# One step of the first chunk's normalisation at each turn of the attention loop, in place of each third

## The chip, the core and the metric

The kernel runs on one core of a Trainium2 chip, in one launch. The metric is device microseconds (us) of that core, from one execution of the whole program; every time below is of that kind. The engines are called by the names of the profile: PE multiplies matrices, DVE is the vector engine, ACT the scalar engine, POOL is GpSimd, and SP issues transfers. Each engine runs its own list of instructions strictly in order, and waits on semaphores for the others.

## What is computed

Three parts follow each other. The first is causal attention with a decay, for 4 batches and 8 heads of 576 positions and 64 channels; its output is 4 x 576 rows of 512 channels. The second takes the real part of a two-dimensional Fourier transform, normalises each row, and runs a feed-forward layer. The third mixes tokens and channels. In short:

```python
scores = scale * q @ k.T + decay          # causal, 32 heads of 576 x 576
x = softmax(scores) @ v                   # -> (4, 576, 512)
u = x + real(fft(fft(x, axis=1), axis=2))
un = (u - mean(u)) / sqrt(var(u) + 1e-6)
x = u + relu(un @ w_ch1) @ w_ch2
theta = x @ w_theta
y = w_tok_r @ (x * cos(theta)) + w_tok_i @ (x * sin(theta))
out = (x + y) + relu((x + y) @ w_ch)
```

## The kernel before, in words

The sum `u` is kept whole in fast memory, with the 512 channels on 4 x 128 partitions and the 2304 rows along the free axis. The feed-forward part cuts these rows into 6 chunks of 384 (`CH`), numbered 0 to 5.

**The attention loop** (`phase1`) walks over the heads n = -1 to 33. In each round it keeps three heads in flight: the scores of head n+1 (`score_units`, matrix products at lines 215 and 216; on DVE the row minimum at 220 and 223; the exponential on ACT at 228; a scaling on DVE and POOL at 240), the transposes of head n-1 (`turn_units`, PE line 258, copies at 262 and 264), and the product with the values of head n-2 (`av_units`, PE line 276). When a pair of heads is complete, ACT copies it out (`evac_pair`, lines 291 to 307, with a small transfer and the two vector instructions 305 and 307). When a batch is complete, its Fourier sums are computed by `fft_units`: the products at lines 360 and 371 from the tiles `eh`, `el`, `oh`, `ol` (made at 333 to 342), then those at 388, and the result goes to `u`.

A round of the loop has 6 turns, and each turn calls `pull()`, which advances three generators by one step where it may: the rows of `evac_pair`, the normalisation `norm`, and the Fourier sums `fft`. Chunk 0 lies in batch 0 and is complete long before; its normalisation generator is made in the round n = 29, after the third batch's Fourier sums have been drained. Rounds 29 to 33 have 30 turns.

**The normalisation** of one chunk (`norm_units`, then `norm_end`) has 20 steps: three sums on POOL (lines 637 to 639); the mean by PE (643) and the differences on DVE (645); squares on ACT (648) and their sums on POOL (649, 651), twice; a wait of eight empty steps; the variance by PE (656) and the root on ACT (663); two empty steps; the reciprocal on DVE (666) and its spread over the partitions by PE (668); and then four steps, each with a product on DVE (675), a copy on ACT (676) and a remainder on DVE (677). The last two make the tile `un`. What is left of the generator when the loop ends is drained in one piece (`for _ in norm`).

**The weights** of the feed-forward part come as 64-bit numbers, and `decode` makes two float32r parts of each (`wf`): on DVE lines 519, 523, 527, 531, 534 and, for most, 535; on ACT 520, 522, 532; on POOL 536 and 538. `load(k)` queues the two halves of the weights of unit k. From round 31 on, `fill(2)` advances this queue by two steps in each turn.

**The feed-forward part** (`phase2`) first drains the last batch's Fourier sums and then runs its units: `ffn1` (PE line 688, 12 products, from `un` and `wf`; the two parts of `h` at 693 on ACT and 694 on DVE) and `ffn2` (PE line 702, the sum into `u` at 710 on DVE). The first two `ffn1` need `un` of chunk 0 and the weights of units 0 and 1.

What order the instructions have on each engine is not only that of the code: a scheduler orders them by the code's order, its own costs and `high_priority` marks, so a moved step shifts its neighbours on every engine too.

Of the kernel before, what the change touches and what calls it, by code (L numbers as in the profile page):

```python
# [31 lines left out]
C1 = 6.28125  # L32
C2 = 2.0 * math.pi - 6.28125
MAGIC = 12582912.0
# 64-bit weights, read by their high words as float32 patterns: the least normal float32 (squared)
# and the largest that 12 bits hold.
LEAST2 = (1.125 * 2.0**-15) ** 2
MOST = 122876.0
G = 4
# [2 lines left out]
def f(ap):  # L42
    return ap.bitcast(F32)


class Net:
# [31 lines left out]
    def bank_t(self):  # L78
        return self.pst.tile([128, 1024], F32, tag="t", name="pt")

# [1 line left out]
    def p1_open(self):  # L82
        nc, tc = self.nc, self.tc
        self.p1f, self.p1a, self.p1b, self.pu0 = (ExitStack() for _ in range(4))
# [330 lines left out]
    def phase1(self):  # L415
        pair, heads = self.p1_open()
        NH = B * H
        pairs, heads, raws = {0: pair}, dict(enumerate(heads)), {}
        T, EO, fft = None, None, None
        self.tick = 0  # L420
        rows, norm = iter(()), iter(())

        def pull():
            nonlocal fft
            next(rows, 0)
            self.tick += 1
            if self.tick % 3 == 0:
                next(norm, 0)
            if (self.tick % 5 or n > 24) and fft is not None and next(fft, 0) == 0:
                fft = None  # L430

        for n in range(-1, NH + 2):
            a = self.score_units(heads[n + 1], (n + 1) % 2) if n + 1 < NH else iter(())
            prep = iter(())
            if n + 2 < NH:
                p, g = divmod(n + 2, 2)
                if n >= 0:
                    heads[n + 2] = dict(pair=pairs[p], g=n + 2)
                    prep = self.prep_units(n + 2, pairs[p], raws.pop(n + 2), heads[n + 2])
                if g == 1 and p + 1 < B * NP:  # L440
                    pairs[p + 1] = self.load_pair(p + 1)
            if n + 3 < NH:
                raws[n + 3] = self.load_head(n + 3)
            c = iter(())
            m = n - 2
            if m >= 0:
                pm, gm = divmod(m, 2)
                hm = pm % NP
                if gm == 0:
                    T = self.bank_t()  # L450
                    if hm == 0:
                        E = self.c1.tile([128, 2, S], F32, tag="E", name="E", bufs=2)
                        O = self.c1.tile([128, 2, S], F32, tag="O", name="O", bufs=2)
                        EO = (E, O)
                c = self.av_units(heads[m], gm, T)
            t = self.turn_units(heads[n - 1]) if 1 <= n <= NH else iter(())
            if n == NH - 1:
                self.p1a.close()
                self.p2_open()
                self.load(0)  # L460
                self.load(1)
            k = n - 2
            if 0 <= k < 4:
                for j in range(2):
                    self.load_dft(2 * k + j, f(heads[n]["hi"][0:1, 0, 0:2]))
            if n == NH - 3:
                while fft is not None:
                    pull()
                t1 = self.c1.tile([128, 2, CH], F32, tag="E", name="uc1", bufs=2)
                t2 = self.c1.tile([128, 2, CH], F32, tag="O", name="uc2", bufs=2)  # L470
                t3 = self.c1.tile([128, 2, CH], F32, tag="yh", name="s12", bufs=1)
                t4 = self.c1.tile([128, 2, CH], F32, tag="yl", name="sq", bufs=1)
                t5 = self.c1.tile([128, 4], F32, tag="zh", name="rs", bufs=1)
                norm = self.norm_units(0, ((t1, t2), t3[:, 0], t3[:, 1], t4, t5))
            live = True
            while live:
                live = False
                for g_ in [(a, c, t)[i] for i in [2, 1, 0]]:
                    if next(g_, 0) is None:
                        live = True  # L480
                next(prep, 0)
                pull()
                if n >= NH - 1:
                    self.fill(2)
            for _ in prep:
                pass
            if m >= 0 and gm == 1:
                for _ in rows:
                    pass
                rows = self.evac_pair(EO[0], EO[1], hm, T)  # L490
                next(rows)
                if hm == NP - 1:
                    fft = self.fft_units(pm // NP, *EO)
        for _ in norm:
            pass
        self.p1b.close()
        for _ in rows:
            pass
        self.pt.close()
        self.pso = self.ctx.enter_context(self.tc.tile_pool(name="pso", bufs=2, space=PSUM))  # L500
        return fft

# [1 line left out]
    def decode(self, place, src, n):  # L504
        nc, w = self.nc, self.x1
        raw = w.tile([128, 512, 2], I32, tag="raw", name="raw", bufs=2)
        nc.sync.dma_start(
            raw[:, 0:n], src.bitcast(I32).rearrange("p (n t) -> p n t", t=2)
        )
        self.nraw += 1  # L510
        me = self.nd
        self.nd += 1
        low, high = raw[:, 0:n, 0], raw[:, 0:n, 1]
        yield
        dst = place()
        a = w.tile([128, 512], F32, tag="sq", name="a", bufs=3)[:, 0:n]
        t = w.tile([128, 512], I32, tag="t", name="t", bufs=3)[:, 0:n]
        square, tail = f(dst[:, 0]), f(dst[:, 1])
        nc.vector.tensor_scalar(a, f(high), MOST, -MOST, ALU.min, ALU.max)  # L519
        nc.scalar.activation(dst[:, 1], low.bitcast(U32), AF.Copy, scale=2.0**-52)  # L520
        self.nraw -= 1
        nc.scalar.activation(dst[:, 0], a, AF.Square)
        nc.vector.tensor_scalar(
            t, a.bitcast(I32), 3, 0x3FFFFFF8, ALU.logical_shift_left, ALU.bitwise_and
        )
        yield
        nc.vector.scalar_tensor_tensor(
            t, a.bitcast(I32), -0x40000000, t, ALU.bitwise_and, ALU.bitwise_or
        )
        yield  # L530
        nc.vector.scalar_tensor_tensor(a, square, LEAST2, f(t), ALU.is_ge, ALU.mult)  # L531
        nc.scalar.copy(dst[:, 0], a)
        yield
        nc.vector.tensor_scalar(t, a.bitcast(I32), -0x00800000, None, ALU.bitwise_and)  # L534
        (nc.gpsimd if me in [4, 6] else nc.vector).tensor_tensor(dst[:, 1], tail, f(t), ALU.mult)  # L535
        nc.gpsimd.tensor_tensor(a, a, f(dst[:, 0]), ALU.subtract)  # L536
        yield
        nc.gpsimd.tensor_tensor(dst[:, 1], a, tail, ALU.add)
        yield
# [45 lines left out]
        while self.step(g) is None:  # L585
            pass

# [1 line left out]
    def p2_open(self):  # L589
        nc, tc = self.nc, self.tc  # L590
        self.pw, self.px2 = ExitStack(), ExitStack()
        self.x1 = self.pw.enter_context(tc.tile_pool(name="x1", bufs=1, side="right"))
        self.wf = {}
        self.queue, self.raws, self.loads = deque(), deque(), {}
        self.nraw = self.nd = 0
        self.active = 3
# [188 lines left out]
        while self.queue:  # L785
            self.fill(1)

# [1 line left out]
    def load_big(self, into, name, k):  # L789
        def place():  # L790
            into.append(self.wtile("x" if name == "wth" else "w"))
            return into[-1]

        self.later(self.decode(place, self.i[name][k], 512))
# [326 lines left out]
```

## Time and profile before

| what | value |
|---|---|
| time, median of 3 runs (lowest to highest) | 1077.78 us (1076.75 to 1079.5) |
| span of the profiled execution, from the first to the last instruction | 1078.3 us |
| PE busy, matrix products | 1007.1 us (93%) |
| DVE busy | 770.6 us (71%) |
| POOL busy | 515.0 us (48%) |
| ACT busy | 480.9 us (45%) |
| chain that ended last | PE 65%, DVE 24%, issue 6%, ACT 3%, POOL 2% |

The profile gives the span of one profiled execution and no other time for it; it lies 0.5 us above the median of the runs. Busy time is what an engine spends inside instructions, and matrix products overlap, so a busy PE need not be at its peak. The chain that ended last is followed back from the last instruction, at each step to what released it. A share over the whole span mixes stages with different limits; the stage around the change is read apart, in the rows below.

### The profile page before, as it was taken

The page shows a single profiled execution, that of the slowest core. Times are in us where ns is not written, and L with a number is a line of the kernel's source. Part 1 is how long each engine was busy: PE and PEld are TensorE (multiplying, and loading weights), DVE is VectorE, ACT ScalarE, POOL GpSimd, SP SyncE. Part 2 cuts the span into 40 slices and gives each one's busy share as a digit, 9 for nine tenths or more (in the row PEclk, how much of TensorE's full clock was granted, in tenths as well). Part 3 has the DMA queues.
Part 4 walks back from the last instruction along what each step waited for, and adds up shares of the span by engine and source line. Part 5 has one row for each costly group of instructions (what it writes and reads, how often), then busy time and mean ns, then how long its engine had stood idle before and what let it go on. Part 6 is the DMA issues. An engine that isn't in the chain of part 4 may idle for free.

```text
span 1078.3 us, 16568 instructions
## 1 busy us (share of the span) xinstructions
PE 1007.1 (93%) x5880; PEld 896.2 (83%) x5880; DVE 770.6 (71%) x1767; ACT 480.9 (45%) x1151; POOL 515.0 (48%) x560
## 2 busy tenths in 40 slices
PE   3999999999997898999999999999789999999998
PEld 1676777766765687899999999989688999999998
DVE  7678988877778878766454555589989675666654
ACT  5677866755646443242222222234334453434331
POOL 5666757646566447443222222236637463635321
PEclk9989999998899889799999999999989999999999
DMA  4453223322204111011111111113221000000001
GB/s 157 136 167 116 95 89 101 101 75 71 93 25 137 40 59 40 1 40 40 40 40 40 40 40 40 40 64 103 67 64 59 1 1 34 12 23 23 12 35 44
DMA packets 21910, 64.78 MB, mean 60 GB/s; under 512 B 3286, under 2 KB 6614, under 8 KB 21828
## 3 DMA queue, kind: packets, MB, share of 16 engines
q1 hardware_dynamic: 18100, 59.36, 16.7%
q0 software_dynamic: 3008, 3.20, 1.2%
q10 hardware_dynamic: 720, 1.18, 0.3%
q8 instruction: 46, 0.75, 0.3%
q14 instruction: 36, 0.29, 0.1%
HBM read 58.83 MB, written 4.87 MB: 59 GB/s over the span
## 4 chain that ended last, share of the span: by engine, by line
PE 65%; DVE 24%; issue 6%; ACT 3%; POOL 2%; ACTq 0%; DVEq 0%; POOLq 0%
PE pa L688 11%; PE pt L276 9%; PE pb L258 7%; PE pb L702 6%; PE po L702 5%; PE pb L901 4%; PE pa L912 4%; PE pa L865 3%; PE pa L215 3%; PE pa L216 3%; PE pb L388 3%; PE po L901 3%; DVE wf L535 2%; DVE a L519 2%; DVE a L531 2%
## 5 line engine op out<-in xcount | busy, mean ns | idle before, releaser
L688 PE MATMUL pa<-un,wf 128*128 128x384 f32 x1152 | 228.4, 348 | 6.6 <-ACT un L676 5.6
L688 PEld LDWEIGHTS pa<-un,wf 128*128 128x128 f32 x1152 | 210.7, 197 | 10.0 <-ACT un L676 6.3
L536 POOL TENSOR_TENSOR a<-a,wf 128x512 f32<-128x512 f32 x40 | 67.6, 1691 | 192.9 <-DVE t L534 174.7
L702 PE MATMUL pb<-h,wf 128*128 128x384 f32 x660 | 138.6, 342 | 11.3 <-DVE u L710 9.7
L694 DVE SCALAR_TENSOR_TENSOR h<-pa,h 128x384 fp32r<-128x384 f32 x96 | 53.0, 552 | 122.6 <-ACT h L693 122.5
L276 PE MATMUL pt<-PT,v 128*128 128x320 f32 (+4 forms) x448 | 132.2, 402 | 0.5 <-ACT O L292 0.5
L702 PEld LDWEIGHTS pb<-h,wf 128*128 128x128 f32 x660 | 117.6, 190 | 14.4 <-DVE u L710 12.1
L228 ACT ACTIVATE P<-pa,mn 64x512 f32<-64x512 f32 (+4 forms) x192 | 97.6, 513 | 62.3 <-DVE mn L223 56.0
L693 ACT ACTIVATE h<-pa 128x384 fp32r<-128x384 f32 x96 | 46.7, 488 | 174.8 <-PE pa L688 174.7
L702 PE MATMUL po<-h,wf 128*128 128x384 f32 x492 | 107.2, 347 | 15.3 <-DVE u L710 11.3
L702 PEld LDWEIGHTS po<-h,wf 128*128 128x128 f32 x492 | 89.5, 194 | 17.5 <-DVE u L710 12.6
L240 POOL TENSOR_SCALAR P<-P,rz 128x128 f32<-128x128 f32 (+3 forms) x128 | 83.0, 664 | 43.7 <-DVE rz L237 30.3
L258 PE MATMUL pb<-ident,P 128*128 128x128 f32 (+2 forms) x480 | 101.7, 292 | 1.5 <-POOL P L240 1.2
L215 PE MATMUL pa<-hi 128*64 128x512 f32 (+2 forms) x192 | 79.6, 421 | 20.7 <-ACT P L228 10.9
L901 PE MATMUL pb<-wtk,z 128*128 128x288 f32 x513 | 97.0, 294 | 0.0
L258 PEld LDWEIGHTS pb<-ident,P 128*128 128x128 f32 (+2 forms) x480 | 60.0, 141 | 42.6 <-issue 19.2
L891 POOL TENSOR_TENSOR z<-kra,z 128x256 fp32r<-128x256 f32 x72 | 53.8, 767 | 86.8 <-ACT z L890 86.8
L276 PEld LDWEIGHTS pt<-PT,v 128*128 128x128 f32 (+1 forms) x448 | 75.3, 197 | 23.5 <-issue 8.0
L220 DVE TENSOR_REDUCE mn<-pa 64x1 f32<-64x512 f32 (+3 forms) x128 | 59.8, 479 | 37.9 <-PE pa L216 36.9
L901 PEld LDWEIGHTS pb<-wtk,z 128*128 128x128 f32 x513 | 79.2, 188 | 0.0
L901 PE MATMUL po<-wtk,z 128*128 128x288 f32 x351 | 75.1, 295 | 1.0 <-POOL z L891 1.0
L215 PEld LDWEIGHTS pa<-hi 128*128 128x128 f32 (+1 forms) x192 | 36.2, 189 | 35.1 <-ACT P L228 14.5
(197 smaller groups left out, 2063.8 us busy)
## 6 DMA issues: line engine op xcount, KB each, us to landing
raw<-in_qk SPq DMA_DIRECT2D x31, 576.0 KB, 3.7
raw<-in_wf SPq DMA_DIRECT2D x32, 512.0 KB, 3.6
v<-in_vp SPq DMA_DIRECT2D x16, 640.0 KB, 4.4
raw<-in_wtk SPq DMA_DIRECT2D x18, 288.0 KB, 2.9
out<-ob SPq DMA_DIRECT2D x12, 288.0 KB, 2.1
dft<-in_dft POOLq DMA_DIRECT2D x8, 346.0 KB, 3.7
raw<-in_wth SPq DMA_DIRECT2D x4, 512.0 KB, 3.7
raw<-in_wch SPq DMA_DIRECT2D x4, 512.0 KB, 3.5
```

The costliest lines, as they stand in the source:

```text
L215: nc.tensor.matmul(t[:m, 0 : b - a], hi[:, 1, n0 : n0 + m], hi[:, 0, a:b], start=True, stop=False)
L220: nc.vector.tensor_reduce(mn[:m, i : i + 1], ps[:m, 0:n0], mybir.AxisListType.X, ALU.min)
L228: nc.scalar.activation(P[:m, POFF[i] + a : POFF[i] + b], t[:m, 0 : b - a], AF.Exp, bias=lowest, scale=-1.0, accum_out=zs[:m, i + k : i + k ...
L240: (nc.vector if k in [3] else nc.gpsimd).tensor_scalar(P[:m, o : o + w], P[:m, o : o + w], rz[:m, k : k + 1], 1.0, ALU.mult, ALU.mult)
L258: nc.tensor.transpose(ps[:kw, off % 512 : off % 512 + qw], src, self.ident[:qw, :qw])
L276: nc.tensor.matmul(T[:, 256 + a : 256 + hi_q], v[:kw, j, g, :], PT[:kw, PTOFF[j] + a - 128 * j : PTOFF[j] + hi_q - 128 * j], start=(g == 0 ...
L536: nc.gpsimd.tensor_tensor(a, a, f(dst[:, 0]), ALU.subtract)
L688: nc.tensor.matmul(ps[:, 0:CH], t[:, l, 128 * d : 128 * d + 128], un[r][:, d], start=n == 0, stop=n == 11)
L694: nc.vector.scalar_tensor_tensor(h[:, 1], ps[:, 0:CH], 0.0, f(h[:, 0]), ALU.max, ALU.subtract)
L702: nc.tensor.matmul(outs[d], t[:, l, 128 * d : 128 * d + 128], h[:, r], start=k % G == 0 and n == 0, stop=k % G == G - 1 and n == 2,)
L891: nc.gpsimd.tensor_tensor(z[:, 1], t, f(z[:, 0]), ALU.subtract)
L901: nc.tensor.matmul(acc[k][th], z[:, l, 128 * k : 128 * k + 128], self.wtk[kt][:, r, 288 * th : 288 * th + 288], start=first and i == 0 and ...
```

## The change

`pull()` now advances the normalisation of chunk 0 at each turn and no longer at each third. Only chunk 0 has its normalisation there; those of the chunks 1 to 5 are advanced by the queue of `phase2`. In 30 turns the generator made 10 of its steps before, and the rest was drained behind the loop. Now all 20 are made by the turn 20 of 30, so nothing is left to drain. The rest of the diff takes out comments. One line less in `pull()` moves every line behind it up by one: what is line 688 in the profile of before is 687 in the changed kernel.

```diff
         def pull():
             nonlocal fft
             next(rows, 0)
             self.tick += 1
-            if self.tick % 3 == 0:
-                next(norm, 0)
+            next(norm, 0)
             if (self.tick % 5 or n > 24) and fft is not None and next(fft, 0) == 0:
                 fft = None
```

The scheduler makes of this another order on every engine, from the scores of head 30 to the second chunk of the feed-forward part; behind that the orders are equal again. Three places of it follow. A name `pt` is the sum of a pair of heads, `pa` and `pb` are other banks, `po` an output bank of `ffn2`.

On PE, the mean of chunk 0 in the kernel before stands behind the first scores of head 31 (`q_97`):

```order
L215 MATMUL pa<-hi 64x64
L216 MATMUL pa<-kl,q_97 64x64
L643 MATMUL pb<-s_3187,mean 128x384
L215 MATMUL pa<-hi 128x512
L216 MATMUL pa<-kl,q_97 128x512
```

and now, within the scores of head 30 (`q_96`):

```order
L215 MATMUL pa<-hi 128x256
L216 MATMUL pa<-kl,q_96 128x256
L642 MATMUL pb<-s_3187,mean 128x384
L215 MATMUL pa<-hi 128x128
L216 MATMUL pa<-kl,q_96 128x128
```

The mean moved one head forward, ahead of the last score product of head 30.

On PE at the end of the attention, before (the last L276 belong to head 31):

```order
L656 MATMUL pb<-mean,s_3187 128x1 x3
L276 MATMUL pt<-PT,v 128x256
L276 MATMUL pt<-PT,v 128x320
L276 MATMUL pt<-PT,v 128x128
L276 MATMUL pt<-PT,v 128x320 x2
L276 MATMUL pt<-PT,v 128x192
L276 MATMUL pt<-PT,v 128x64
L668 MATMUL pb<-ident,rs 128x128 x3
L688 MATMUL pa<-un,wf 128x384 x24
L702 MATMUL po<-h,wf 128x384 x7
L360 MATMUL pb<-dft,eh 128x258 x2
```

and now:

```order
L687 MATMUL pa<-un,wf 128x384 x8
L276 MATMUL pt<-PT,v 128x256
L276 MATMUL pt<-PT,v 128x320
L276 MATMUL pt<-PT,v 128x128
L276 MATMUL pt<-PT,v 128x320 x2
L276 MATMUL pt<-PT,v 128x192
L276 MATMUL pt<-PT,v 128x64
L687 MATMUL pa<-un,wf 128x384 x14
L701 MATMUL po<-h,wf 128x384 x4
L360 MATMUL pb<-dft,eh 128x258 x2
```

Ten of the 24 products of the first two `ffn1` (two more stand further up) moved ahead of the last head's product with the values, and the steps L656 and L668 are now further up.

On DVE behind the last scaling of the attention (L240), before:

```order
L240 TENSOR_SCALAR P<-P,rz_94 128x512
L264 COPY PT<-pb 64x64
L519 TENSOR_SCALAR a<-raw 128x512
L523 TENSOR_SCALAR t<-a 128x512
L527 SCALAR_TENSOR_TENSOR t<-a,t 128x512
L519 TENSOR_SCALAR a<-raw 128x512
L531 SCALAR_TENSOR_TENSOR a<-wf,t 128x512
```

and now:

```order
L240 TENSOR_SCALAR P<-P,rz_94 128x512
L518 TENSOR_SCALAR a<-raw 128x512
L522 TENSOR_SCALAR t<-a 128x512
L665 RECIPROCAL rs<-rs 128x3
L526 SCALAR_TENSOR_TENSOR t<-a,t 128x512
L518 TENSOR_SCALAR a<-raw 128x512
L530 SCALAR_TENSOR_TENSOR a<-wf,t 128x512
L522 TENSOR_SCALAR t<-a 128x512
L674 TENSOR_TENSOR uc_3185<-uc_3185,pb 128x384
L526 SCALAR_TENSOR_TENSOR t<-a,t 128x512
L264 COPY PT<-pb 64x64
```

The reciprocal (665) and the products of the normalisation (674, and 676 behind them) now alternate with the decoding of the weights, where they stood behind four halves of it.

## Rows read from the trace of the kernel before

**Rows 1.** Busy time by stretch: bounds, length, five engines (instructions), TensorE clock, DMA share, GB/s
```profile
340.00:360.00 20.00, 10.94 (x46) 8.04 (x45) 18.80 (x29) 9.62 (x19) 12.82 (x9) 0.83 0.17 54
345.00:445.00 100.00, 84.19 (x416) 74.35 (x416) 85.58 (x145) 38.28 (x74) 56.60 (x46) 0.83 0.16 48
370.00:385.00 15.00, 15.00 (x56) 10.93 (x54) 9.26 (x21) 2.48 (x5) 9.68 (x7) 0.66 0.13 37
404.00:443.00 39.00, 31.41 (x158) 30.04 (x157) 35.35 (x54) 10.77 (x21) 25.87 (x22) 0.83 0.08 28
```

**Rows 2.** Timeline of PE at the seam: start, duration, instruction, count, idle before
```profile
332.10 2.58 PE L258 MATMUL pb<-ident,P 128*128 128x128 f32 x14
...
339.39 3.20 PE L276 MATMUL pt<-PT,v 128*128 128x256 f32 x14
344.17 0.93 PE L668 MATMUL pb<-ident,rs 128*128 128x128 f32 x6 [1.57 <-DVE rs L666]
350.67 1.01 PE L688 MATMUL pa<-un,wf 128*128 128x384 f32 x2 [5.57 <-ACT un L676]
...
360.73 0.46 PE L360 MATMUL pb<-dft,eh 128*128 128x258 f32 x2
```

**Rows 3.** Timeline of DVE over the same stretch, ends of it and quiet instructions
```profile
327.68 0.49 DVE L240 TENSOR_SCALAR P<-P,rz 128x512 f32<-128x512 f32 x1
330.25 0.22 DVE L264 COPY PT<-pb 64x64 f32<-64x64 f32 x1 [2.08 <-PE pb L258]
...
331.30 0.69 DVE L527 SCALAR_TENSOR_TENSOR t<-a,t 128x512 int32<-128x512 int32 x1
...
333.18 0.42 DVE L534 TENSOR_SCALAR t<-a 128x512 int32<-128x512 int32 x1
...
334.11 0.68 DVE L535 TENSOR_TENSOR wf<-wf,t 128x512 fp32r<-128x512 f32 x1
...
355.07 0.80 DVE L305 TENSOR_TENSOR O<-E,sh 1x576 f32<-1x576 f32 x1
...
356.96 0.75 DVE L307 TENSOR_TENSOR E<-E,sh 1x576 f32<-1x576 f32 x1
...
360.97 0.75 DVE L340 TENSOR_TENSOR el<-ee,eh 128x580 fp32r<-128x580 f32 x1
```

**Rows 4.** Timeline of DVE, instructions that took longer
```profile
339.54 1.82 DVE L305 TENSOR_TENSOR O<-E,sh 1x576 f32<-1x576 f32 x1
...
342.02 1.67 DVE L307 TENSOR_TENSOR E<-E,sh 1x576 f32<-1x576 f32 x1
...
345.19 1.48 DVE L519 TENSOR_SCALAR a<-raw 128x512 f32<-128x512 f32 x1 [1.08 <-POOL wf L538]
346.59 2.42 DVE L523 TENSOR_SCALAR t<-a 128x512 int32<-128x512 int32 x2
...
351.87 1.77 DVE L535 TENSOR_TENSOR wf<-wf,t 128x512 fp32r<-128x512 f32 x1
```

**Rows 5.** Timeline of POOL: a sum of the normalisation, two steps of a weight
```profile
314.00 1.00 POOL L639 TENSOR_TENSOR s<-s 128x384 f32<-128x384 f32 x1
...
334.55 4.79 POOL L536 TENSOR_TENSOR a<-a,wf 128x512 f32<-128x512 f32 x1 [4.41 <-ACT wf L532]
339.42 1.33 POOL L538 TENSOR_TENSOR wf<-a,wf 128x512 fp32r<-128x512 f32 x1
```

**Rows 6.** Timeline of PE, head 30 and the mean of the first chunk
```profile
312.59 0.38 PE L216 MATMUL pa<-kl,q 66*128 66x256 f32 x1
...
317.68 0.89 PE L643 MATMUL pb<-s,mean 128*128 128x384 f32 x2
```

**Rows 7.** Timeline of DVE, head 30 and the first chunk
```profile
313.84 0.30 DVE L223 CUSTOM_DVE_ANT_0 pa<-pa,mask 128x128 f32<-128x128 f32 x1
...
320.23 1.00 DVE L645 TENSOR_TENSOR uc<-u,pb 128x384 f32<-128x384 f32 x2
```

**Rows 8.** Timeline of PE, a unit of the feed-forward part
```profile
430.13 2.26 PE L702 MATMUL po<-h,wf 128*128 128x384 f32 x6 [3.12 <-ACT h L693]
```

## The prediction

> **What bounds the kernel now.** I read the busy time of long stretches first. The 100 us behind the attention are the stretch that the change touches: PE is busy for 84.19 us there at a mean granted clock of 0.83, and DVE for 85.58 us [rows 1]. So neither engine is full, and PE loses time in two ways, by standing still and by running at the lower of its two clock levels (1.2 in place of 2.4 GHz).
>
> Then the timeline of PE at the seam. The attention's last product ends at 342.59 (339.39 + 3.20), and the Fourier sums of the last batch begin at 360.73 [rows 2]. Between 340 and 360 PE is busy for 10.94 of 20 us, so it stands for 9.06 us; the longest piece, 5.57 us, waits for `un` of chunk 0 [rows 1, 2]. This is the gap that an earlier normalisation could fill.
>
> Then the timeline of DVE over the same time, which decides. DVE is busy for 18.80 of those 20 us [rows 1]. From the end of its last scaling at 328.17 (327.68 + 0.49) to the end of `el` at 361.72 (360.97 + 0.75), which the Fourier sums need, pass 33.55 us [rows 3], of which DVE stands still only 2.08 + 1.08 = 3.16 us [rows 3, 4]. PE's gap is thus DVE's queue seen from PE: the products of the normalisation, the decoding of four weight halves and the last rows of the attention stand there one behind the other.
>
> **The change part by part.** It removes and adds no work: the three sums on POOL, the four differences, the root, the four products and four remainders and their matrix products are all issued, only earlier. No transfer is among the 20 steps. The first weight's transfers leave when head 31's last score is done, so they shift with it.
>
> *The mean, one head earlier.* L643 now stands behind the 256-column score of head 30, which ends at 312.97 (312.59 + 0.38) [rows 6]; with the product of 320 columns that moved ahead of that score, PE comes to it at about 313.4. Its input is POOL's last sum, ready at 315.00 [rows 5]. PE waits 1.6 us with the whole score chain behind it. Behind it on DVE stand four differences (1.00 for two, so 2.0) ahead of head 30's last row minimum, which ran at 313.84 and now can't before about 317.6 [rows 7]. The last scaling is therefore late by 1.6 us (PE's wait alone) to 3.8 us (317.6 - 313.84, all of the minimum's delay). I take 2.4: the wait, and part of the eight more transposes (2.58 / 14 = 0.18 each, 1.5 in all) that now stand ahead of head 31's 384-column score, since two products of the values moved behind it [rows 2]. **+2.4.**
>
> *DVE from the last scaling to `el`.* The list holds the same instructions and one L527 more, 0.6 us [rows 3]. The 3.16 us of waiting go, since `decode` now begins without the copy that was waited for. New waits appear: DVE is at the first product of the normalisation (674) after seven short instructions, about 3 us, while PE reaches the spread (667) only behind ten transposes and three products of head 30, about 1.8 + 1.4, and needs 0.93 itself [rows 2]. I put these waits at 1.7 us: one of 1.4 there and 0.3 for the root. Sum 0.6 - 3.16 + 1.7 = **-0.9**, between -2.6 (no new wait) and +0.6 (as much as before).
>
> *What DVE loses to POOL.* In that stretch single DVE instructions took 1.82, 1.67, 1.48, 2.42 (two) and 1.77 us [rows 4], where the same forms otherwise take 0.80, 0.75, 0.42, 0.84 and 0.68 [rows 3]: 5.7 us more. POOL was in a step of a weight each time, and in its turn needed 4.79 us for a step of some 1.3 while DVE ran without a pause [rows 5]. Four weight halves bring eight such steps before and after; I take the same loss, so **0**, and price the worse case below. The Trainium skill, "SBUF — State Buffer", section "Who interferes with whom", has the rule for this: a vector instruction with two operands in SBUF, or in a mode of two ports, and a GpSimd instruction exclude each other for the whole of the instruction. The rows agree, since 1.82 against 0.80 is one step of POOL waited out. By that rule taken strictly the change would be slower, not neutral; that is the third rival.
>
> *PE at the seam.* The 24 products of the first two `ffn1` fill waits further up, but what is won there is not won at the end: L360 still stands behind `el` and L694. The eight products that moved ahead of head 31's last product wait for a weight and for the third remainder (676). I expect that product some 6 to 9 us later than 342.59, and it is hidden still: its copies are due only when DVE reaches L305, which ran at 355.07 [rows 3]. If that cover goes, the loss is what the copies come too late, up to 2 us. The Fourier sums so begin at 360.7 + 2.4 - 0.9 = 362.2.
>
> *The Fourier sums and the low clock.* In the 15 us from 370 PE is busy throughout at a mean granted clock of 0.66, which costs 15 x 0.34 = 5.1 us [rows 1]. PE stands for some microseconds ahead of these sums in both kernels, so I expect such a stretch again: **0**, between -5.1 (it is gone) and +5.1 (a second one).
>
> *The first chunks of the feed-forward part.* From 404 to 443 PE is busy 31.41 of 39 us and DVE 35.35 [rows 1]; the longest wait, 3.12 us, is for `h`, which stood behind a weight step that waited for DVE [rows 8]. Up to `el` and through the Fourier sums DVE now does one L527 and one step like it (L531) more, so it has 2 x 0.6 us less to do here: **-1.2**, between 0 and -1.2 as far as work goes; waits can move by about one of the size above.
>
> Sum: 2.4 - 0.9 + 0 + 0 - 1.2 = +0.3 us on 1078.3, thus 1078.6. The profiled execution lies 0.5 us over the median of 1077.78, so I predict **1078.1 us**.
>
> **The rivals.**
>
> *The gap closes (faster).* If POOL's steps fall where DVE reads from PSUM or waits, the 9.06 us of standing PE go and only the late scores remain: 1077.8 - 9.06 + 2.4 = 1071.1. For it speaks that the largest wait named `un`; against it that DVE was busy 18.80 of 20 us there [rows 1]. Chance 0.12.
>
> *No low clock in the Fourier sums (faster).* The products now spread over the end of the attention could leave PE busier in the time ahead of them. That gives 1078.1 - 5.1 = 1073.0. Against it: DVE still lets PE wait directly ahead of L360. Chance 0.15.
>
> *DVE and POOL in strict turns (slower).* Now DVE's list between the first L534 and the last L535 of these weights has no idle time, and eight POOL steps of 1.33 us [rows 5] stand against it. If each is waited out in full, the loss is 10.6 and not 5.7 us, thus +4.9: 1083.0. It decides from the point where more than six or seven of the eight steps are waited out, which makes the delay more than 3 us. This is the page's rule, worked out from rows. Chance 0.18.
>
> *A second stop in the first chunks (slower).* The new DVE order there decodes two halves in step, so that the next L519 waits for POOL's L538 with L694 and L710 queued behind it. One more wait like the 3.12 us one, with a low clock behind it as in 404 to 443 (0.83, half of one such loss, 39 x 0.17 / 2 = 3.3), gives 1078.1 + 6.4 = 1084.5; it is slower than no change from the moment that wait exceeds the 1.2 us won. Chance 0.12.
>
> That the change doesn't do what it says can be set aside: the order on PE shows the steps moved.
>
> **How the numbers follow.** The forecast has the chance 0.43, the two faster rivals 0.12 + 0.15, the two slower ones 0.18 + 0.12. A difference of 0.3%, 3.2 us, is about what a measurement of this kernel can tell from no change, so faster is 0.27, same 0.43, slower 0.30. The forecast's own range, from its bounds, is 1075 to 1081. To leave out no more than 2 in 10, the range takes in most of both sides, down to 1071.5 and up to 1084.
>
> **What would show it.** Right: the mean runs near 315 behind an idle PE of about 1.6 us; the last scaling of DVE ends at 330 to 331; head 31's product ends at 348 to 352; L360 begins at 360 to 364 behind a waiting PE; DVE's lengthened instructions still sum to about 6 us; a low clock within the Fourier sums. Wrong: L360 before 358 (DVE was not the bound), or after 365 (strict turns), or a difference that arises only behind 404.

## The result, and the profile after

The changed kernel takes 1095.52 us (median of 4 runs, 1092.73 to 1098.55), the kernel before 1078.64 us on the same chip (4 runs, 1076.75 to 1080.96). The ratio is 1.014, with an interval from 1.0107 to 1.0172: slower by 16.9 us. The prediction, 1078.1 us and at most 1084, was wrong. The profiled execution of the change took 1092.73 us with a span of 1090.9, so a time holds 1.8 us outside the span; the two profiled spans differ by 12.6 us. All comparisons are between executions in the chip's fast state; for that, one of the ten runs of x13 below is left out.

Times below are compared from one instruction that both traces have, the first row minimum (line 220) of head 30, which begins at 308.82 before and at 305.59 now; what lies ahead of it is the same in both kernels, and merely ran 3.2 us faster in the profiled execution of the change. A line of `decode` or of the normalisation has in the change one number less than before.

| stretch | before, us | now, us | difference | forecast |
|---|---|---|---|---|
| head 30's minimum to the end of the last scaling (240) | 19.35 | 20.18 | +0.8 | +2.4 |
| to the end of `el` (340) | 33.54 | 33.85 | +0.3 | -0.9 |
| to the end of the Fourier products (388) | 16.80 | 18.12 | +1.3 | 0 |
| to the end of chunk 0 (its fourth 709) | 29.45 | 38.66 | +9.2 | -1.2 for both chunks |
| to the end of chunk 2 (the twelfth 709) | 47.43 | 48.97 | +1.5 | |
| to the end of the span | 622.94 | 625.55 | +2.6 | 0 |

In these two executions each of the three stretches at the seam came within 2 us of its forecast; what the seam's order costs by itself is told with the runs x1 and p2. The loss comes behind it, most of it before chunk 0 is done. Behind chunk 2 the order is the same in both kernels, and the 2.6 us there aren't traced to a wait: from 700 us on the granted clock is 0.96 in the change and 0.97 before. The busy time by stretch of the change (the columns as in [rows 1]: bounds, length, five engines with their instructions, TensorE clock, DMA share, GB/s) shows it:

```profile
345.00:445.00 100.00, 77.19 (x377) 68.75 (x377) 83.43 (x132) 35.41 (x66) 53.81 (x40) 0.82 0.15 48
354.00:370.00 16.00, 12.40 (x47) 10.03 (x48) 14.02 (x24) 7.22 (x15) 10.27 (x7) 0.50 0.26 92
388.00:401.00 13.00, 11.88 (x47) 11.88 (x48) 6.36 (x8) 1.89 (x5) 4.09 (x3) 0.50 0.26 81
439.00:452.00 13.00, 8.47 (x31) 8.50 (x32) 6.72 (x13) 0.26 (x1) 4.83 (x5) 0.50 0.01 1
```

In the 100 us from 345, PE is busy 7 us less than before (77.19 against 84.19 [rows 1]) and DVE 2 us less: both wait more. Three stretches run at 0.50, the lower clock level. In the kernel before, the same view gives for the last two of these stretches, and for the one at its own stop of 3.12 us:

```profile
388.00:401.00 13.00, 13.00 (x73) 12.41 (x74) 10.33 (x21) 6.07 (x14) 7.11 (x5) 0.87 0.18 53
430.00:443.00 13.00, 10.27 (x35) 9.80 (x36) 12.26 (x18) 0.87 (x3) 6.74 (x7) 0.50 0.00 1
439.00:452.00 13.00, 12.21 (x62) 11.95 (x63) 8.06 (x16) 4.42 (x8) 4.84 (x6) 0.85 0.00 1
```

So the kernel before has 13 us at 0.50 beside its stop at 430 too, and the low clock at the change's second stop is not new. The timeline of PE in the change shows what PE did ahead of each stretch:

```profile
311.58 0.91 PE L642 MATMUL pb<-s,mean 128*128 128x384 f32 x2 [1.54 <-POOL s L638]
...
347.65 2.69 PE L687 MATMUL pa<-un,wf 128*128 128x384 f32 x14
...
357.59 1.01 PE L701 MATMUL po<-h,wf 128*128 128x384 f32 x2 [6.29 <-DVE h L693]
358.39 0.63 PE L360 MATMUL pb<-dft,eh 128*128 128x258 f32 x2
...
384.05 0.34 PE L701 MATMUL po<-h,wf 128*128 128x384 f32 x1
389.12 1.65 PE L687 MATMUL pa<-un,wf 128*128 128x384 f32 x4 [4.73 <-POOL wf L537]
...
392.70 4.26 PE L625 MATMUL pb<-mean,sq 128*128 128x1 f32 x20
...
398.89 1.48 PE L667 MATMUL pb<-ident,rs 128*128 128x128 f32 x6
...
443.53 1.94 PE L701 MATMUL po<-h,wf 128*128 128x384 f32 x5 [9.38 <-DVE u L709]
```

The first line is the mean, which waits 1.54 us for POOL's sum. PE then stops three times: for 6.29 us ahead of the Fourier sums, where it had stood in several pieces before ([rows 2], the longest 5.57); for 4.73 us at 389; and for 9.38 us at 443, where one of 3.12 us [rows 8] and one of 2.60 us stood before. Each has low clock beside it. The same work around 389 in the kernel before:

```profile
389.00 2.29 PE L626 MATMUL pb<-mean,sq 128*128 128x1 f32 x20
...
392.00 1.50 PE L668 MATMUL pb<-ident,rs 128*128 128x128 f32 x6
393.15 3.33 PE L688 MATMUL pa<-un,wf 128*128 128x384 f32 x11
```

There the variance of chunk 1 (626) and the spread of its root (668) come first, and the products of unit 3 after them, when the weight is ready. In the change the scheduler put ten products of unit 3 (687) ahead of the variance (625). They wait for the weight; the variance stands behind them and runs at half clock (4.26 us against 2.29), and so the spread (667) comes 10.1 us later, counted from head 30 (93.3 against 83.2). The other engines show the rest (timelines of the change: DVE, then ACT and POOL, and a row of POOL in the kernel before):

```profile
380.91 2.10 DVE L530 SCALAR_TENSOR_TENSOR a<-wf,t 128x512 f32<-128x512 f32 x2
382.93 1.24 DVE L533 TENSOR_SCALAR t<-a 128x512 int32<-128x512 int32 x1
...
386.46 1.48 DVE L518 TENSOR_SCALAR a<-raw 128x512 f32<-128x512 f32 x1
387.87 1.75 DVE L534 TENSOR_TENSOR wf<-wf,t 128x512 fp32r<-128x512 f32 x1
389.54 1.50 DVE L522 TENSOR_SCALAR t<-a 128x512 int32<-128x512 int32 x1
...
397.29 0.18 DVE L665 RECIPROCAL rs<-rs 128x3 f32<-128x3 f32 x1 [4.84 <-ACT rs L662]
...
435.84 1.21 DVE L518 TENSOR_SCALAR a<-raw 128x512 f32<-128x512 f32 x1
440.64 1.47 DVE L518 TENSOR_SCALAR a<-raw 128x512 f32<-128x512 f32 x1 [3.59 <-POOL wf L537]
442.04 0.41 DVE L522 TENSOR_SCALAR t<-a 128x512 int32<-128x512 int32 x1
442.37 0.54 DVE L693 SCALAR_TENSOR_TENSOR h<-pa,h 128x384 fp32r<-128x384 f32 x1
442.84 1.01 DVE L709 TENSOR_TENSOR u<-po,u 128x384 f32<-128x384 f32 x2
```

```profile
397.00 0.26 ACT L662 ACTIVATE rs<-pb,eps 128x3 f32<-128x3 f32 x1 [8.39 <-PE pb L625]
```

```profile
380.99 1.47 POOL L636 TENSOR_TENSOR s<-u 128x384 f32<-128x384 f32 x1
...
387.74 1.33 POOL L537 TENSOR_TENSOR wf<-a,wf 128x512 fp32r<-128x512 f32 x1
...
390.84 1.33 POOL L537 TENSOR_TENSOR wf<-a,wf 128x512 fp32r<-128x512 f32 x1
407.33 1.25 POOL L648 TENSOR_TENSOR s<-sq 128x384 f32<-128x384 f32 x1 [15.17 <-ACT sq L647]
...
436.73 2.66 POOL L535 TENSOR_TENSOR a<-a,wf 128x512 f32<-128x512 f32 x2
439.36 2.48 POOL L537 TENSOR_TENSOR wf<-a,wf 128x512 fp32r<-128x512 f32 x2
```

```profile
391.38 1.29 POOL L538 TENSOR_TENSOR wf<-a,wf 128x512 fp32r<-128x512 f32 x1
```

From 381 to 392 POOL works almost without a pause, and DVE's steps 533, 518, 534 and 522 take 1.24 to 1.75 us where 0.41 to 0.68 is usual [rows 3]. Yet the weight isn't late for that: counted from head 30, POOL's first 537 for it ends at 83.5 us in the change, and the 538 of before ended at 83.9. What is new is that PE's list asks for it sooner. ACT and DVE then wait for the late variance (8.39 and 4.84 us), and POOL stands for 15.17 us until the squares behind it on ACT come. At 440 comes the other stop: two halves are decoded in step, the second 518 waits 3.59 us for POOL's 537, and behind it in DVE's list stand 693 and the 709 for which PE waits.

### The profile page after: what moved, and what is told of

The parts are those of the page before. It is cut to its first block, busy times and chain, and to the rows that moved or that the text cites. A ratio compares the mean times of both kernels' runs of the same rounds, so it can differ in the third digit from the quotient of the medians.

```text
span 1090.9 us, 16560 instructions
## 1 busy us (share of the span) xinstructions
PE 1011.2 (93%) x5880; PEld 902.1 (83%) x5880; DVE 781.6 (72%) x1767; ACT 482.3 (44%) x1151; POOL 509.1 (47%) x560
## 4 chain that ended last, share of the span: by engine, by line
PE 55%; DVE 23%; issue 5%; POOL 3%; ACT 3%; DMA 1%; ACTq 0%; DVEq 0%; POOLq 0%; SPq 0%
PE pa L687 11%; PE pb L701 6%; PE po L701 5%; PE pt L276 5%; PE pb L900 4%; PE pa L911 4%; PE pb L258 4%; PE pa L864 3%; PE po L900 3%; DVE wf L534 2%; DVE a L518 2%; PE pb L388 2%; DVE t L533 2%; DVE t L526 2%; DVE a L530 2%
## 5 line engine op out<-in xcount | busy, mean ns | idle before, releaser
L687 PE MATMUL pa<-un,wf 128*128 128x384 f32 x1152 | 225.9, 344 | 4.7 <-POOL wf L537 4.7
L687 PEld LDWEIGHTS pa<-un,wf 128*128 128x128 f32 x1152 | 207.8, 194 | 6.7 <-POOL wf L537 5.0
L276 PE MATMUL pt<-PT,v 128*128 128x320 f32 (+4 forms) x448 | 133.0, 404 | 2.1 <-ACT O L292 1.9
L701 PE MATMUL po<-h,wf 128*128 128x384 f32 x492 | 109.5, 351 | 26.1 <-DVE u L709 19.4
L701 PEld LDWEIGHTS pb<-h,wf 128*128 128x128 f32 x660 | 120.1, 194 | 15.6 <-DVE u L709 12.0
L701 PEld LDWEIGHTS po<-h,wf 128*128 128x128 f32 x492 | 90.8, 196 | 28.8 <-DVE u L709 11.4
L240 POOL TENSOR_SCALAR P<-P,rz 128x128 f32<-128x128 f32 (+3 forms) x128 | 83.0, 663 | 43.4 <-DVE rz L237 29.9
L276 PEld LDWEIGHTS pt<-PT,v 128*128 128x128 f32 (+1 forms) x448 | 75.5, 198 | 25.9 <-issue 8.7
L864 PE MATMUL pa<-wf,xs 128*128 128x256 f32 x456 | 64.8, 292 | 0.0
```

What stands on the lines that cost most here:

```text
L240: (nc.vector if k in [3] else nc.gpsimd).tensor_scalar(P[:m, o : o + w], P[:m, o : o + w], rz[:m, k : k + 1], 1.0, ALU.mult, ALU.mult)
L276: nc.tensor.matmul(T[:, 256 + a : 256 + hi_q], v[:kw, j, g, :], PT[:kw, PTOFF[j] + a - 128 * j : PTOFF[j] + hi_q - 128 * j], start=(g == 0 ...
L687: nc.tensor.matmul(ps[:, 0:CH], t[:, l, 128 * d : 128 * d + 128], un[r][:, d], start=n == 0, stop=n == 11)
L701: nc.tensor.matmul(outs[d], t[:, l, 128 * d : 128 * d + 128], h[:, r], start=k % G == 0 and n == 0, stop=k % G == G - 1 and n == 2,)
L864: nc.tensor.matmul(th, xs[:, l, d], self.wth[d][:, r, 256 * hf : 256 * hf + 256], start=n == 0, stop=n == 11)
```

## The experiments

**How an order is put back.** All experiments below but p2 and x15 hold an order written down by line and count. `hold` runs ahead of the scheduler and chains the instructions of each engine:

```diff
         net.phase3()
+        hold(net, tc)
...
+    for engine, text in ORDER.items():
+        chain = [found[(engine, *map(int, t.split(".")))] for t in text.split()]
+        for a, b in zip(chain, chain[1:]):
+            tc.add_manual_dep(b, a.name, info, reason="order")
```

The held stretch begins on each engine about where the last Fourier sums do, on PE with the fourteen products of `ffn1` directly ahead of them ("behind the seam"), and ends where both kernels' orders are equal again: 361 instructions on PE, 119 on DVE, 61 on ACT, 40 on POOL.

**What was measured.** "Against before" is the ratio to the kernel before on the same chip, with its interval. "Clock" is span x (1 - mean granted clock), the mean over a kernel's runs, less the same for the kernel before beside it; "other" is that difference for span x clock. What the clock column counts is half of the time at the lower level, also where PE stands in that time: in the change's second stop PE stands for 4.5 of the 13 us shown at 0.50. It is an account, and x10 is the test. The last two columns are from the profiled run: from the end of `el` to that of chunk 0, and from there to the end of chunk 2.

| run | median, us | against before | clock | other | `el` to chunk 0 | to chunk 2 |
|---|---|---|---|---|---|---|
| kernel before | 1078.6 to 1080.5 | 1 | 0 | 0 | 46.25 | 47.43 |
| c_after, the change held | 1097.17 | 1.0142 (1.0103 to 1.0182) | +14.8 | +1.7 | 56.78 | 48.97 |
| x1 | 1086.68 | 1.0065 (1.0032 to 1.0098) | +4.3 | +2.8 | 50.97 | 47.46 |
| x2 | 1096.19 | 1.0153 (1.0099 to 1.0208) | +11.9 | +5.1 | 56.90 | 48.84 |
| x3 | 1092.43 | 1.0131 (1.0075 to 1.0187) | +12.6 | +2.0 | 56.17 | 48.83 |
| x4 | 1086.88 | 1.0069 (1.004 to 1.0098) | +8.0 | 0.0 | 59.50 | 46.66 |
| x6 | 1078.39 | 0.9984 (0.9958 to 1.001) | +0.2 | -1.4 | 49.28 | 48.77 |
| x8 | 1094.02 | 1.011 (1.0063 to 1.0157) | +12.7 | +0.2 | 57.39 | 44.07 |
| x9 | 1091.85 | 1.0089 (1.006 to 1.0119) | +8.8 | +1.7 | 47.54 | 51.01 |
| p2 | 1077.34 | 0.9987 (0.9962 to 1.0013) | +0.5 | -2.0 | 44.60 | 47.35 |
| x10 | 1088.19 | 1.0088 (1.0053 to 1.0123) | +3.6 | +5.8 | 54.46 | 45.06 |
| x13 | 1091.02 | 1.01 (1.0065 to 1.0134) | +1.9 | +9.0 | 56.91 | 44.98 |
| x14 | 1079.35 | 1.0006 (0.9973 to 1.0039) | -1.5 | +1.8 | 45.91 | 47.58 |
| x15 | 1076.62 | 0.9967 (0.9943 to 0.9992) | -1.7 | -1.8 | 46.02 | 47.44 |

**c_after.** The change's own order, held. It is the control.

```diff
+    "PE": "687.9 687.10 687.11 687.13 687.14 ..."
```

> The changed kernel with its own order written down and held: the control for the other runs on this chip. Every theory: as the change, 1092 to 1097 us. Another time would mean that holding an order costs something by itself.

1097.17 us, as the change. Holding an order costs nothing by itself.

**x1: the change's seam, the order of before behind it.**

```diff
-    "PE": "687.9 687.10 687.11 687.13 687.14 ..."
+    "PE": "687.13 687.14 687.15 687.16 687.17 ..."
```

(and likewise on DVE, ACT and POOL)

> The changed kernel with its own order up to the start of the last Fourier sums, and behind that point, on PE, DVE, ACT and POOL, the order of the kernel before. Theory 'behind' (the loss is made by the order of the first feed-forward chunks, by the two stops of PE at 389 and 443 and the low clock after each): 1078 to 1082 us, about +1 on the kernel before, with no wait above 4 us on PE between 385 and 450. Theory 'seam' (the 6.29 us stop ahead of the Fourier sums and what follows it make the loss): 1092 to 1096, as the change. Theory 'POOL' (DVE and POOL hold each other up over the whole stretch): in between, 1085 to 1090.

1086.68 us, between the theories. Of the 16.7 us, 9.3 go with the order behind the seam, and PE's longest waits between 385 and 450 are 3.43 and 3.15 us. About 7 us stay, which theory "behind" had not expected.

**x2: the mirror image**, the seam of before with the change's order behind it.

```diff
         net.phase3()
+        hold(net, tc)
...
+    "PE": "688.9 688.10 688.11 688.13 688.14 ..."
```

> The mirror image: the kernel before up to the start of the last Fourier sums, and behind that point the order of the changed kernel on the four engines. Theory 'behind': 1092 to 1096 us, with both stops of PE (at about 389 and 443) and the low clock after each. Theory 'seam': 1077 to 1080, as the kernel before. Theory 'POOL': 1083 to 1090.

1096.19 us: the whole loss, with the seam untouched. The profiled run has the stops of 4.73 and 9.38 us. The order behind the seam is enough by itself; the seam's 7 us in x1 don't add to it. Why they don't was not tried.

**x3: PE alone in the order of before.**

```diff
-    "PE": "687.9 687.10 687.11 687.13 687.14 ..."
+    "PE": "687.13 687.14 687.15 687.16 687.17 ..."
     "DVE": "530.4 518.5 533.4 522.5 518.6 ..."
```

> The changed kernel with PE alone in the order of the kernel before, behind the start of the last Fourier sums (there the last products of ffn1 of unit 3 stand behind the variance and the root of chunk 1 and no longer ahead of them). Theory 'behind', if its first stop (4.73 us, for the second half of unit 3's weight) carries its share: 5 to 9 us less than the change, 1087 to 1091, and no PE wait for the weight at 389. If only the second stop (9.38 us) matters, or the seam: within 2 us of the change, 1093 to 1097.

1092.43 us, and in the trace nothing is won up to chunk 0 (56.17 us). The first stop only moves, from PE to DVE (timeline of DVE in x3):

```profile
399.48 0.56 DVE L693 SCALAR_TENSOR_TENSOR h<-pa,h 128x384 fp32r<-128x384 f32 x1 [4.75 <-ACT h L692]
399.95 1.47 DVE L674 TENSOR_TENSOR uc<-uc,pb 128x384 f32<-128x384 f32 x3
```

DVE's list has unit 3's 693 ahead of the products 674 of the normalisation, as PE's list had unit 3's products ahead of the variance. PE now does the variance first, and DVE waits for unit 3 with 674 queued behind. As read from these rows, it is one decision written on two engines, and putting back one half wins little.

**x4: the change's order, with four buffers for the first temporary of the decoding.**

```diff
-        a = w.tile([128, 512], F32, tag="sq", name="a", bufs=3)[:, 0:n]
+        a = w.tile([128, 512], F32, tag="sq", name="a", bufs=4)[:, 0:n]
```

(the change's order is held as well, and the tile `z` of the last part, which shares these buffers, is spread over them anew)

> The changed kernel with its own order held, and four in place of three buffers for the first temporary of the weights' decoding, so that the line 518 of a half waits for the POOL step 537 of the fourth half before and not the third. Theory 'behind', if its second stop comes from that wait (3.59 us of DVE at 440.64 with 693 and 709 queued behind it): 4 to 9 us less than the change, 1087 to 1092, and PE waits less than 6 us at 443. If DVE would have waited there for something else, or the seam makes the loss: within 2 us of the change.

1086.88 us: 7.6 over the kernel before beside it, where c_after, with the same order and three buffers, has 16.7 on another chip. In the trace the two steps 518 at 438.28 run without a wait, and PE waits 6.81 us and not 9.38:

```profile
438.28 2.62 DVE L518 TENSOR_SCALAR a<-raw 128x512 f32<-128x512 f32 x2
440.81 1.48 DVE L522 TENSOR_SCALAR t<-a 128x512 int32<-128x512 int32 x1
442.21 0.55 DVE L693 SCALAR_TENSOR_TENSOR h<-pa,h 128x384 fp32r<-128x384 f32 x1
```

The mechanism of the second stop is as read. The size is less sure: the profiled run was the slowest of the ten and shows only 2.3 us less from chunk 0 to chunk 2, and the 9 us won are more than the second stop is worth by x8 and x9 below. What else the buffer wins in this order is open.

**x8 and x9: one stop each.** x8 has the change's order up to the end of chunk 0 and that of before behind it; x9 the reverse. On DVE the orders meet at the last 709 of chunk 0 (709.3):

```diff
-    "DVE": "... 693.5 709.0 709.1 709.2 665.2 709.3 526.8 526.9 530.8 530.9 ..."
+    "DVE": "... 709.1 709.2 674.8 674.9 709.3 674.10 693.6 676.8 674.11 676.9 ..."
```

(x9 with -, x8 with +)

> The change's order up to the end of chunk 0 (the last 709 of that chunk), and the order of the kernel before behind it, on four engines. It has the stop at 389 and lacks the one at 443. Theory 'first stop' (what is lost is lost by the end of chunk 0; the second stop gives its 5 us back one chunk later, since from the end of chunk 0 to that of chunk 2 the change takes 48.97 us and the kernel before 47.43): 0 to 3 us less than the change, 1092 to 1096. Theory 'both stops' (9.38 us against 3.12 + 2.60): 4 to 8 us less, 1087 to 1091.

> The change's seam, then the order of the kernel before up to the end of chunk 0, then the change's order again: it lacks the stop of 4.73 us for the POOL step and has the one at 443. Theory 'first stop': as x1 and 1 to 2 us more, 1086 to 1090. Theory 'both stops': 4 to 8 us more than x1, 1091 to 1095.

x8 is 3.2 us below the change, near what "first stop" said; x9 is 4.0 us above x1 when each is set against its own kernel before (11.4 and 7.4), nearer "both stops". The first stop (x8 less x1, 13.5 - 7.4) is then worth about 6 us, the second about 4; by the intervals each is sure to some 5 or 6 us only, so which is dearer isn't shown. Together they make about the 9.3 us between c_after and x1. The column `el` to chunk 0 sorts the runs: where the change's order holds there, 54.5 to 59.5 us (x3, with PE alone put back, among them); where that of before does, 44.6 to 51.0.

**x6: the kernel before, held, with four buffers.**

```diff
+        hold(net, tc)
...
-        a = w.tile([128, 512], F32, tag="sq", name="a", bufs=3)[:, 0:n]
+        a = w.tile([128, 512], F32, tag="sq", name="a", bufs=4)[:, 0:n]
```

> The kernel before with its own order held, and four buffers for the first temporary of the weights' decoding. Theory 'buffers help by themselves' (the fourth buffer takes waits of DVE for POOL away in every chunk, so that x4's gain says nothing of the change's order): 3 to 8 us less than the kernel before, 1071 to 1076. Theory 'buffers help only the order in step': within 2 us of the kernel before.

1078.39 us, 0.9984 with 1 in its interval: the buffer helps the order in step, and hardly that of before.

**p2: half the pace.** The simplest test of the parts: the normalisation still comes early, but the scheduler's order behind the attention stays that of before.

```diff
-            next(norm, 0)
+            if self.tick % 2 == 0:
+                next(norm, 0)
```

> The normalisation of chunk 0 advanced at each second turn. The scheduler then moves the mean into head 30 too, about as in the change, but behind the last product of the attention its order on PE, DVE, ACT and POOL is that of the kernel before. Theory 'order behind': 1078 to 1083 us, no stop of PE above 4 us between 385 and 450. Theory 'earlier mean' (the late scores of head 30 and the clock after them carry x1's 7 us): as x1, 1085 to 1089. Theory 'seam' (the decoding mixed with the normalisation between the last scaling and the last Fourier sums carries them; that order is not in this kernel): as 'order behind'.

1077.34 us: no loss. The test is less clean than it was meant to be: here the mean stands behind head 30's last score product and doesn't wait, where in the change it stands ahead of that product and waits 1.54 us. So p2 doesn't try the mean's place in the change; up to the last scaling the change is 0.8 us late. From the last transposes on, p2 has the order of before. What p2 shows is that the normalisation can come earlier without a loss, and it leaves the seam's order as the likely source of x1's 7 us, which isn't shown by a run of its own. There x1 has PE's wait of 6.29 us in one piece and then 0.50 of clock (first line, x1 from 356). In p2 no wait of PE between the last product of the attention and the Fourier sums is above 2.3 us, and DVE is busy 92.42 of 100 us (second line); the third line is p2's mean:

```profile
356.00:372.00 16.00, 12.18 (x47) 10.10 (x48) 10.89 (x20) 5.89 (x12) 7.71 (x6) 0.50 0.17 61
```

```profile
345.00:445.00 100.00, 84.28 (x438) 74.83 (x437) 92.42 (x151) 39.27 (x75) 58.60 (x45) 0.89 0.15 48
```

```profile
317.10 0.91 PE L643 MATMUL pb<-s,mean 128*128 128x384 f32 x2
```

**x10 and x13: work without use in PE's stops.** x10 fills the stops at 389 and 443, x13 also the one ahead of the Fourier sums.

```diff
-        return h
+        spare(self, t, un); return h
...
+SPARE = {3: 24, 10: 48}
...
+    for _ in range(SPARE.get(unit, 0)):
+        net.nc.tensor.matmul(ps[:, 0:CH], net.wf[(unit - 1) % 4][0][:, 0, 0:128], un[0][:, 0], start=True, stop=True)
```

(x13: `SPARE = {1: 32, 3: 24, 10: 48}`)

> The change in its own order, with products that nobody reads in PE's two stops: 24 of 384 columns ahead of the product that stands 4.73 us at 389, and 48 ahead of the one that stands 9.38 us at 443 (0.17 us each, so 4.1 and 8.2 us, a little less than the stops). Theory 'clock' (the stops cost mostly by the low clock behind them; by the runs so far the change loses 13 to 15 us more to a lower granted clock than the kernel before, and 2 to 3 us to all else): the 13.7 us of half clock behind each of the two stops go, 10 to 14 us less than the change, 1082 to 1086, with the waits of DVE as long as before. Theory 'waits' (the stops cost by their own length): as the change, 1093 to 1097, or more.

> As x10, and 32 more such products (5.4 us) in the stop of 6.29 us ahead of the last Fourier sums. Theory 'clock': the 17.1 us of half clock in the Fourier sums go too, 5 to 9 us less than x10, 1075 to 1081. Theory 'waits': as the change, 1093 to 1097.

x10 is 1088.19 us: 8.1 over the kernel before beside it, where the held change has 16.7. DVE's wait at 441 is as long as in the change (3.68 against 3.59 us), but the stretches at the two filled stops don't run at 0.50 any more (busy time by stretch, x10):

```profile
388.00:401.00 13.00, 12.37 (x73) 12.06 (x72) 10.89 (x16) 5.30 (x10) 6.83 (x5) 0.87 0.25 81
439.00:452.00 13.00, 11.74 (x71) 11.34 (x70) 9.85 (x19) 2.45 (x6) 7.42 (x7) 1.00 0.00 1
```

The loss by clock falls from 14.8 to 3.6 us, and "other" grows by 4.1. So 7 to 9 of the 16.7 us went while the waits that make the stops stayed: of what the two stops cost (9.3 us), the greater part was clock, as far as these intervals can tell. x13 won nothing on top (1091.02): the low clock moved from the start of the Fourier sums to behind their middle, and "other" grew by 3.2. The expectation for it failed.

**x14: the same idea on the kernel before.**

```diff
+SPARE = {10: 9, 11: 7}
...
+        net.nc.tensor.matmul(ps[:, 0:128], net.mean, net.mean, start=True, stop=True)
```

> The kernel before in its own order, with products that nobody reads ahead of its stops at 430 (3.12 us, 9 of 128 columns) and 440 (2.60 us, 7 of them). Theory 'clock': the 13.7 us of half clock from 429 to 443 go, 4 to 7 us less than the kernel before, 1072 to 1075, which would beat both kernels. Theory 'waits': 1078 to 1082.

1079.35 us, 1.0006: what the clock gave (1.5) the products took (1.8). Here, with stops of 3 us, a fill won nothing.

**x15: half pace and four buffers** together.

> The kernel at half pace (a step at each second turn) with four buffers for the first temporary of the decoding; its order on PE and DVE is that of the kernel at half pace. It puts together the two edits that measured a little below the kernel before (ratios 0.9987 and 0.9984, both intervals holding 1). If each is a real gain and they add: 1075 to 1077 us, ratio 0.996 to 0.998 with an interval below 1. If both were chance: within 2 us of the kernel before, and nothing here beats it.

```diff
-            next(norm, 0)
+            if self.tick % 2 == 0:
+                next(norm, 0)
...
-        a = w.tile([128, 512], F32, tag="sq", name="a", bufs=3)[:, 0:n]
+        a = w.tile([128, 512], F32, tag="sq", name="a", bufs=4)[:, 0:n]
```

1076.62 us, 0.9967 (0.9943 to 0.9992), 12 runs against 17. This version is below both kernels, below the kernel before by about 2.8 us; a gain that small is at the edge of what can be told.

## Why the prediction was wrong

*The mean, +2.4: right in kind.* PE waits 1.54 us for POOL's sum (forecast 1.6). The last scaling is 0.8 us late, below the 1.6 to 3.8 that were given: of the wait about half was passed on, and the 0.8 us for the transposes don't show. Why is not traced.

*DVE to `el`, -0.9: +0.3, within its bounds, but by luck.* The waits that were to go did, and only 0.50 us of new ones came where 1.7 were forecast. DVE is busy for 33.06 of 33.85 us there, before for 30.20 of 33.55: 0.6 us for the further step and over 2 us of instructions that took longer, which the next term had put at nothing. The two errors cancel.

*DVE's loss to POOL, 0: too small, at the seam and behind it.* Counting what the decoding steps take over 0.41 and 0.68 us, the loss from 328 to 361 is 4.3 us before and 4.8 now; over all of DVE's instructions the growth is the 2 us just named. From 380 to 408 the decoding steps lose 2.1 us before and 7.0 now. I had placed the third rival at the seam only. Behind it POOL's sums and DVE's decoding met at 381 to 392, and steps of 0.41 to 0.68 us took 1.24 to 1.75. By the Trainium skill, "SBUF — State Buffer", section "Who interferes with whom", an instruction of DVE that needs the ports it shares with GpSimd and one of GpSimd that needs them lock each other out for a whole instruction, wherever they overlap. The trace agrees in these steps (1.24 to 1.75 us). That this loss cost time is not shown: the weight that PE waits for at 389 came no later than before.

*PE at the seam, 0: right for these two executions.* Head 31's product ends 8.4 us later (forecast 6 to 9) and is hidden. The Fourier sums begin 0.9 us later (forecast 1.5). With the order of before behind it, though, the change's seam loses 7 us (x1), for which the prediction has no term.

*The low clock in the Fourier sums, 0 (-5.1 to +5.1): within its bounds.* The 16 us from 354 at 0.50 cost 8.0 us, where 5.1 were priced; the stretch to the end of 388 grew by 1.3 us.

*The first chunks, -1.2 (0 to -1.2): the step that failed.* It measured +9.2 us up to the end of chunk 0, +1.5 up to chunk 2 and +2.6 behind, 13.3 of the 15.7 us that the table above adds up to (the last 2.6 where the orders are equal again). I weighed how much work DVE has there and not in which order it stands. The order was at hand: PE's list of the change has unit 3's products ahead of chunk 1's variance, and DVE's has unit 3's `h` ahead of chunk 1's products. x2 shows that this order alone makes the loss (16.9 us), p2 that an earlier normalisation without it makes none.

*The fourth rival, 0.12 at 1084.5.* Its mechanism came as described, at 440: a step 518 waits for POOL's 537, with 693 and 709 queued behind it. Its price, 6.4 us, was near the second stop's 4; the first stop and the seam's order were not in it. The point that I said would show the forecast wrong, a difference that arises behind 404, was nearly right: it begins at 384.

*What I had priced at the stops' length* is for the greater part clock: by the account 14.8 of the held change's 16.5 us, and by the test (x10) 7 to 9 of 16.7. A stop of 3.12 us and its clock were priced at 6.4 together; that was the right sort of sum, made for one stop where there were three.

*Open:* which wait of the seam's order makes x1's 7 us, and why they vanish where the change's order follows. In x1's profile 4.7 us of them lie between `el` and the end of chunk 0 (50.97 against 46.25), where the order is that of before, so it is not the seam's length alone. A run that splits the seam was not made.

## What to carry to other kernels

When a scheduler places the work, a moved step is judged by the order that comes out everywhere up to where the orders are equal again, not at the place it was moved to: read each engine's list there for an instruction that will wait with others queued behind it, and read the lists of two engines together. Price a stop of TensorE as its length plus the low clock beside it. And try the intermediate pace: here the same intention at half speed left the order behind the attention alone, and lost nothing.

## What was not expected of the hardware

Over all kernels here, span x mean granted clock (means over a kernel's runs) stays within 1040 and 1052 us, and within 1040 and 1047 without the added products, while the spans go from 1075 to 1095: by this account what sets these kernels apart is for the most part how long TensorE was held at the lower level, though some of that time it stood. And the executions of one kernel spread: the kernel before had 1073.03 to 1085.82 us in one set of 31 runs, with a mean clock of 0.971 in the fastest and 0.962 in the slowest, so a single profile's clock stretches are a sample and not the kernel's own.
